# The start of a list-scheduled kernel ordered by a stored table of ranks

## The chip, the cores and the metric

The kernel runs on one core of a Trainium2 chip. The core has five engines, each of which takes its own instructions strictly in order: TensorE (PE in the profile; PEld is its loading of weights), VectorE (DVE), ScalarE (ACT), GpSimd (POOL) and SyncE (SP), which issues the transfers here. The metric is the device time of one execution in microseconds (us), the median of several runs.

## The reference

Linear attention with a random feature map, then a two-layer feed-forward network over all tokens. B = H = 8, S = 576, head dimension 64, 128 features; 4608 tokens of 512 channels, a hidden width of 2048; all inputs and the output are float32.

```
def phi(x):
    proj = np.einsum('bhsd,df->bhsf', x, w_phi)
    proj = proj - np.max(np.abs(proj), axis=-1, keepdims=True)
    return np.concatenate([np.exp(proj), np.exp(-proj)], axis=-1)
q_p, k_p = (phi(q), phi(k))
kv = np.einsum('bhsf,bhsd->bhfd', k_p, v)
z = np.sum(k_p, axis=2)
num = np.einsum('bhsf,bhfd->bhsd', q_p, kv)
den = np.einsum('bhsf,bhf->bhs', q_p, z)[..., None] + 1e-06
x = (num / den), tokens x (H * D)
h = x @ w_in;  r = np.maximum(h, 0.0);  out = (r * r) @ w_out
```

## The kernel before

**The work.** The attention runs in 32 pairs of heads of one batch, four pairs to a batch (`NPAIR`). The feed-forward part, called MoE in the code, runs in 18 chunks of 256 tokens by 8 steps of 256 hidden channels. A step has a first GEMM (24 matmuls, L986, into a bank pair `ph`), a chain of ReLU and square on ACT (L995, L997, L999) and a subtraction on DVE that makes a high part `gh` and a low part `gl`, and a second GEMM (12 matmuls, L1013, into `po`). A chunk can start when the normalized tokens of its batches are in `ring0` or `ring1`, as a high and a low half (L804 on ACT, L807 on DVE).

**The weights.** `w_in` and `w_out` come in eight blocks each as raw 64-bit data, 1 MB a block (`raw0i` to `raw7i` for `w_in`, `raw0o` to `raw7o` for `w_out`). `prep` turns a block into float32 `u` and then into halves: ACT L453 and L448, DVE L456 and L460; for a block of `w_in` also the largest value on ACT (L477), a power of two as its scale (`power`: a transposing gather on TensorE, L402, into the bank `pn`, then four small steps on DVE, L406 to L410), and the halves `win0` (ACT L481) and `win1` (DVE L483); for a block of `w_out` the halves `wh` (ACT L501) and `wl` (POOL L313 and DVE L508). A raw buffer is reused for a later block, so its load waits on SP until the earlier one was read.

**The first six pairs** (0 to 5, `early`) run before there are tokens for the MoE steps. For a pair p TensorE projects k (L563 for the main part, into banks `po` for pairs 0 to 4 and `pp` for pair 5; L569 for the tail, into `pn`) and q (L680 and L686). DVE finds the largest values and subtracts them (`km`, `e`, `kmt`, `et`: L579, L582, L589, L592; for q `qm`, `pt`: L691, L693), ACT takes the exponentials (L585, L587, L595, L597). TensorE multiplies k's features with v (L619, L624, sums in L652, into `pv`); ACT or DVE copies the result out as `kvs` (L317 or L318), TensorE flips it (L664), the flipped copy is `kz`. TensorE flips q's features in two halves (L714, L718, into `pp`), ACT takes their exponentials `qe` (L723, L725), TensorE makes the numerators (L733, copied out as `n`) and denominators (L750, copied into `sx`). The denominators go by a transfer from `sx` to `den`, DVE takes the reciprocal (L767, L768, `rc`), which goes through memory (`rd`) and back spread over all rows (`rb`); DVE multiplies numerators with `rb` (L785). The later pairs run as one `visit` each among the MoE steps.

**Buffers.** PSUM has one `pn`, one `pv`, one `pp` (two banks), two `ph`, two `po`. One buffer `sx` in SBUF serves the copies of the denominators and, as a place for unwanted output, ACT's L526, which sums |v| for the scale of a batch. So the next user of such a buffer waits until all users of the last one are done, a transfer included.

**The order.** All of this is given as operations to a planner (`Plan`), each with an engine (some with a second engine), a duration, what it depends on, the buffers it uses and a rank. `order` is a list scheduler: it goes through a modelled time and gives each engine that is free the ready operation of the least rank (TensorE adds `STAY` to one that would change its tiling). The order of their modelled starts is the order in which the instructions are then written, engine by engine. The core of it:

```
t = free[e] if ready[e] else max(free[e], waiting[e][0][0])
if best is None or t < best[0]:
    best = t, e
...
if e == "PE":
    pick = min(ready[e], key=lambda x: (x[0] + (STAY if self.ops[x[1]].mode[0] != mode else 0.0), x[1]))
    ready[e].remove(pick)
    op = self.ops[pick[1]]
else:
    op = self.ops[heapq.heappop(ready[e])[1]]
```

Ranks come from the code: a pair p has `PER_PAIR * p` (4.5 p) plus a small number for the place in the pair, block n of the weights `PREP0 + PREP1 * n` (16 + n), MoE step n has `LEAD + n` (36 + n); the MoE work on ACT and DVE has its rank less 1000, which puts it ahead of all else. `improve` takes the 1113 operations with ranks between -50 and 70 (the pairs up to about 15, all weights, the GEMMs of about the first 34 steps), moves the ranks of a twentieth of them at random, makes the order anew and keeps it if the modelled end is no later; it does this 400 times from a fixed seed.

Of the kernel before, what the change touches and what calls it, by code (L numbers as in the profile page):

```python
# [3 lines left out]

# [22 lines left out]
B, H, S, D = 8, 8, 576, 64  # L27
F = 128
NP = H // 2
NPAIR = B * NP  # L30
DM = 512
# [4 lines left out]
T = 256  # L36
# [12 lines left out]
STAY = 6.0  # L49
LATER = 2.0  # L50
BEHIND = 0.0
TRIALS, SEED, MOVED = 400, 1, 70.0
CHANGE = 0.15
RA, RQ, RZ = 1.3, 0.4, 0.3
COLD = 1.15
# [22 lines left out]
class Plan:  # L78
# [59 lines left out]
                    todo.append(a)  # L138
        return False

    def improve(self, trials, seed):

        rnd = random.Random(seed)
        best, plan = None, None
        some = [op for op in self.ops if -50.0 < op.rank < MOVED]
        for n in range(trials):
            moved = rnd.sample(some, len(some) // 20) if n else []
            old = [(op, op.rank) for op in moved]
            for op in moved:
                op.rank += rnd.gauss(0.0, 1.5)  # L150
            order = self.order()
            length = max(op.end for op in self.ops)
            if best is None or length <= best:
                best, plan = length, [(op, op.eng) for op in order]
            else:
                for op, rank in old:
                    op.rank = rank
        for op, eng in plan:
            op.take(eng)
        return [op for op, _ in plan]  # L160

    def order(self):
        for op in self.ops:
# [136 lines left out]
def tile_kernel(ctx, tc, qp, kp, vp, w_phi, w_in, w_out, out):  # L300
    nc = tc.nc
    V, A, G, PE, SP = nc.vector, nc.scalar, nc.gpsimd, nc.tensor, nc.sync
    P = Plan()
# [747 lines left out]
    for p in range(NPAIR):  # L1051
        if p % NP == 0 and p:
            b = p // NP
# [16 lines left out]
        op.after = [x for a in op.after for x in (chunk_done[a[1]] if isinstance(a, tuple) else [a])]  # L1070
    P.close()
    with tc.manual_schedule():
        for op in P.improve(TRIALS, SEED):
            op.fn()


PREP0, PREP1 = 16.0, 1.0
# [27 lines left out]
```

## Time and profile before

| what | value |
|---|---|
| median of 3 runs | 1076.79 us (1075.55 to 1077.38) |
| span of the profiled execution, first to last instruction | 1074.5 us |
| mean granted TensorE clock | 0.986 |
| busy: PE, PEld, DVE, ACT, POOL | 1038.8, 707.2, 738.3, 635.6, 136.4 us |

The profiled execution is known by its span; the median of the runs is 2.3 us above that span. A line of a profile gives the engine, the line of the program, the tile that is written and those that are read, and the idle time ahead of it with what ended it. The line numbers are those of the kernel before. PE's records overlap, so a busy PE means only that it has something in flight; the granted clock (1.00 is full speed) is given by stage.

### The profile page before, as it was taken

The numbers are of one execution on the slowest core, as the hardware profiler recorded it, in microseconds if no ns is written. First come the engines' busy times: TensorE is split into PE (matmuls) and PEld (weight loads), VectorE is DVE, ScalarE is ACT, GpSimd is POOL, SyncE is SP. The second block draws the span as 40 slices with busy tenths as digits, with TensorE's granted clock in tenths as the row PEclk, the third lists the DMA queues.
The fourth block names the chain that finished last, engine by engine and source line by source line (L and its number), as shares of the span: only waits on it lengthen the run. The fifth ranks groups of instructions, "written<-read, shape, count | busy, mean of one in ns | idle before, by whom it ended". The sixth has DMA issues, their size and how long they took to land.

```text
span 1074.5 us, 19722 instructions
## 1 busy us (share of the span) xinstructions
PE 1038.8 (97%) x7762; PEld 707.2 (66%) x7762; DVE 738.3 (69%) x1558; ACT 635.6 (59%) x1132; POOL 136.4 (13%) x66
## 2 busy tenths in 40 slices
PE   7778899999999999999999999999999999999997
PEld 5545566666666666666666666666666666677674
DVE  6688988788868877878878877777787855112111
ACT  6789876666656665656665655666556645333332
POOL 0012211111111111111111101111110111000000
PEclk9988999999999999999999999999999999999998
DMA  9742422131122122222212121112120101000000
GB/s 319 272 136 86 163 91 60 29 95 45 59 58 85 45 76 56 76 56 66 67 56 76 56 62 43 52 52 76 44 63 23 51 13 41 1 20 20 1 20 20
DMA packets 68289, 73.49 MB, mean 68 GB/s; under 512 B 36836, under 2 KB 41828, under 8 KB 68196
## 3 DMA queue, kind: packets, MB, share of 16 engines
q1 hardware_dynamic: 68196, 72.23, 22.0%
q8 instruction: 61, 1.00, 0.4%
q14 instruction: 32, 0.26, 0.1%
HBM read 59.18 MB, written 12.99 MB: 67 GB/s over the span
## 4 chain that ended last, share of the span: by engine, by line
PE 90%; DVE 5%; DMA 3%; issue 1%; ACT 0%; SPq 0%; DVEq 0%; ACTq 0%
PE po L1013 37%; PE ph L986 35%; PE pv L619 5%; PE pp L563 3%; PE pn L837 3%; PE pp L907 3%; PE pv L837 2%; PE pv L624 1%; PE pn L569 1%; DVE wl L508 1%; DMA den<-sx 1%; DMA k<-in_kp_dram 1%; DMA v<-in_vp_dram 1%; DMA rd<-rc 1%; DVE u L460 1%
## 5 line engine op out<-in xcount | busy, mean ns | idle before, releaser
L986 PE MATMUL ph<-ring,win 128*128 128x256 f16 x3456 | 398.1, 273 | 0.0
L986 PEld LDWEIGHTS <-win 128*128 128x128 f16 x3456 | 335.8, 98 | 66.2 <-issue 5.4
L995 ACT ACTIVATE r<-ph,cw 128x512 f32<-128x512 f32 x144 | 98.8, 686 | 221.1 <-PE ph L986 221.0
L313 DVE TENSOR_TENSOR gl<-ph,gh 128x512 bf16<-128x512 f32 x144 | 98.5, 684 | 168.0 <-ACT ph L999 167.4
L920 POOL PARTITION_ALL_REDUCE mx<-pt x52 | 114.2, 2197 | 621.5 <-ACT pt L317 449.9
L1013 PE MATMUL po<-wh,gh 128*128 128x512 f32 x432 | 129.4, 421 | 0.0
L1013 PE MATMUL po<-wl,gh 128*128 128x512 bf16 x432 | 112.8, 384 | 0.0
L1013 PE MATMUL po<-wl,gl 128*128 128x512 bf16 x432 | 110.9, 379 | 0.0
L1013 PEld LDWEIGHTS <-gl 128*128 128x128 bf16 x576 | 56.1, 97 | 69.8 <-issue 0.4
L997 ACT ACTIVATE gh<-r 128x512 fp32r<-128x512 f32 x144 | 90.7, 630 | 6.2 <-PE po L1013 1.7
L1013 PEld LDWEIGHTS <-gh 128*128 128x128 bf16 x576 | 44.9, 98 | 74.7 <-issue 40.3
L1013 PEld LDWEIGHTS po<-wh,gh 128*128 128x128 f32 x432 | 74.5, 190 | 18.7 <-issue 5.4
L999 ACT ACTIVATE ph<-r 128x512 f32<-128x512 f32 x144 | 84.0, 583 | 0.1
L1013 PE MATMUL po<-wout,gh 128*128 128x512 f32 (+1 forms) x288 | 75.8, 404 | 0.0
L317 ACT ACTIVATE n<-pn 128x320 f32<-128x320 f32 (+1 forms) x32 | 13.8, 431 | 100.7 <-PE pn L837 98.4
L619 PE MATMUL pv<-e,v 128*64 128x256 f32 x512 | 63.9, 394 | 0.7 <-ACT kz L317 0.7
L934 DVE SCALAR_TENSOR_TENSOR pt<-qe,zc,pt 128x576 f32<-128x576 f32 x52 | 42.2, 812 | 18.9 <-ACT pt L932 18.2
L313 DVE TENSOR_TENSOR qe<-pt,mx 128x576 f32<-128x576 f32 x52 | 39.2, 755 | 16.8 <-POOL mx L920 16.5
L619 PEld LDWEIGHTS pv<-e,v 128*64 128x64 f32 x512 | 36.9, 142 | 17.8 <-issue 3.6
L585 ACT ACTIVATE e<-e 128x512 f32<-128x512 f32 x64 | 39.7, 621 | 14.6 <-DVE e L582 14.4
L925 ACT ACTIVATE qe<-qe 128x576 f32<-128x576 f32 x52 | 34.9, 671 | 13.9 <-DVE qe L313 13.9
L871 DVE STREAM_TRANSPOSE kvs<-pv 128x256 f32<-128x256 f32 x26 | 11.6, 445 | 44.3 <-PE pv L837 42.4
(206 smaller groups left out, 1394.0 us busy)
## 6 DMA issues: line engine op xcount, KB each, us to landing
v<-in_vp_dram SPq DMA_DIRECT2D x32, 320.0 KB
k<-in_kp_dram SPq DMA_DIRECT2D x32, 288.0 KB
q<-in_qp_dram SPq DMA_DIRECT2D x32, 288.0 KB
rb<-rd SPq DMA_DIRECT2D x64, 144.0 KB
out_dram<-o SPq DMA_DIRECT2D x36, 256.0 KB
td<-kvs SPq DMA_DIRECT2D x26, 128.0 KB
kz<-td SPq DMA_DIRECT2D x208, 16.0 KB
raw0i<-in_w_in_dram SPq DMA_DIRECT2D x1, 1024.0 KB
```

What stands on the lines that cost most here:

```text
L313: eng.tensor_tensor(out=out_, in0=a, in1=b_, op=ALU.subtract)
L585: o = P.add("ACT", act_us(512), lambda n=n: A.activation(out=e_[n][:, :, 1, :], in_=e_[n][:, :, 0, :], func=AF.Exp, scale=-1.0), [o], [("e ...
L619: PE.matmul(out=to[64 * h:64 * h + 64, 0:256], lhsT=v_[p][:, t, h, :], rhs=e_[2 * p + h][:, t].rearrange("p s f -> p (s f)"), start=t == 0 ...
L837: PE.matmul(out=to[64 * h:64 * h + 64, :], lhsT=kz_[n][:, 128 * s_ + 64 * h:128 * s_ + 64 * h + 64], rhs=qe_[2 * n + h].rearrange("p (s x) ...
L920: o = P.add("POOL", par_us(S), lambda n=n, h=h: G.partition_all_reduce(mx_[n], pt_[p][:, h, :], channels=128, reduce_op=bass_isa.ReduceOp. ...
L925: o = P.add("ACT", act_us(S), lambda qe=qe: A.activation(out=qe(1), in_=qe(0), func=AF.Exp, scale=-1.0), [o], [("qe", n)], R(RQ + 0.4))
L934: o = P.add("DVE", dve_us(S), lambda h=h, qe=qe, y=y: V.scalar_tensor_tensor(out=y(), in0=qe(1), scalar=zc_[p][:, 2 * h + 1:2 * h + 2], in ...
L986: PE.matmul(out=ph[:, j, :], lhsT=win[w][:, t, 128 * ff:128 * ff + 128], rhs=ring[half][x][:, t, c0:c0 + T], start=k == 0, stop=k == 3 * K ...
L995: o = P.add("ACT", act_us(512, 1), lambda: A.activation(out=r_[n], in_=ph_[bank], func=AF.Relu, scale=cw[:, f, 0:1]), [g1], [("ph", bank), ...
L997: sq = P.add("ACT", act_us(512), lambda: A.activation(out=gh_[n], in_=r_[n], func=AF.Square), [o], [("r", n), ("gh", n)], Q)
L999: o = P.add("ACT", 0.59, lambda: A.activation(out=ph_[bank], in_=r_[n], func=AF.Square), [o], [("ph", bank), ("r", n)], Q, other=("DVE", 0 ...
L1013: PE.matmul(out=po_[po[i][1]], lhsT=g[:, j, 128 * i:128 * i + 128], rhs=w[:, j, :], start=(ff == 0 and s == 0), stop=(ff == 2 * NFP - 1 an ...
```

## The change

`improve` no longer searches. It reads one rank for each of the same 1113 operations from a string of 2226 characters, two to a rank in base 90, with a step of 0.05, and calls `order` once. Nothing else of the plan changes: the operations, their modelled durations, what they depend on and the buffers are the same, so the same work is done in another order on each engine, and a few operations that may run on either of two engines change sides (ACT has 1091 rows for 1094, DVE 1299 for 1298). The table of 23 lines is cut to its first here.

```
--- before.py
+++ after.py
@@ -1,5 +1,4 @@
 import heapq
-import random
 from contextlib import ExitStack
 
 import numpy as np
@@ -49,7 +48,7 @@
 STAY = 6.0
 LATER = 2.0
 BEHIND = 0.0
-TRIALS, SEED, MOVED = 400, 1, 70.0
+MOVED = 70.0
 CHANGE = 0.15
 RA, RQ, RZ = 1.3, 0.4, 0.3
 COLD = 1.15
@@ -138,26 +137,14 @@
                     todo.append(a)
         return False
 
-    def improve(self, trials, seed):
-
-        rnd = random.Random(seed)
-        best, plan = None, None
+    def improve(self):
+
         some = [op for op in self.ops if -50.0 < op.rank < MOVED]
-        for n in range(trials):
-            moved = rnd.sample(some, len(some) // 20) if n else []
-            old = [(op, op.rank) for op in moved]
-            for op in moved:
-                op.rank += rnd.gauss(0.0, 1.5)
-            order = self.order()
-            length = max(op.end for op in self.ops)
-            if best is None or length <= best:
-                best, plan = length, [(op, op.eng) for op in order]
-            else:
-                for op, rank in old:
-                    op.rank = rank
-        for op, eng in plan:
-            op.take(eng)
-        return [op for op, _ in plan]
+        assert 2 * len(some) == len(RANKS)
+        for n, op in enumerate(some):
+            i, j = (DIGITS.index(x) for x in RANKS[2 * n:2 * n + 2])
+            op.rank = (90 * i + j - 3000) * 0.05
+        return self.order()
 
     def order(self):
         for op in self.ops:
@@ -1070,8 +1057,36 @@
         op.after = [x for a in op.after for x in (chunk_done[a[1]] if isinstance(a, tuple) else [a])]
     P.close()
     with tc.manual_schedule():
-        for op in P.improve(TRIALS, SEED):
+        for op in P.improve():
             op.fn()
+
+
+DIGITS = "".join(chr(c) for c in range(33, 127) if chr(c) not in "\"\\'")[:90]
+RANKS = (
+    "E*I*6};p:FN}3lBSJ8;JD3V-JRBNL&_`XLL^L|OOIhRkK8>VJ&MY[.B)F/SJ>GP{3oD)JXPwHgIUJiayZ#RAP(OxL6OeU>DiI:Sy"
...
+)
 
 
 PREP0, PREP1 = 16.0, 1.0
```

In the new kernel the lines up to the scheduler's end stand 13 lower: its L304 is L317 of before, its L513 is L526. The rows below are those of the two orders; a name ends in a number of its own for each buffer, and the number ahead of it counts the pair (`e_6` and `e_7` are the two heads of pair 3) or the use.

First place: ACT, in the start, around the second denominators' copy into `sx` (`sx_6` before, `sx_5` now) and the copy `kvs_2` that the flip of pair 2 waits for. Before:

```order
L453 ACTIVATE raw0o_364<-raw0o_364 128x1024
L317 ACTIVATE sx_6_570<-pn_9_535 128x288
L585 ACTIVATE e_6_533<-e_6_533 128x4x128
L587 ACTIVATE e_6_533<-e_6_533 128x4x128
L526 ACTIVATE sx_7_587,vm_1_531<-v_5_405 128x640
L317 ACTIVATE kvs_2_593<-pv_5_508 128x384
L723 ACTIVATE qe_4_598<-pp_4_580 128x2x288
L585 ACTIVATE e_7_591<-e_7_591 128x4x128
L725 ACTIVATE qe_4_598<-pp_4_580 128x2x288
```

The same place on ACT now:

```order
L304 ACTIVATE sx_5_541<-pn_8_500 128x288
L710 ACTIVATE qe_4_545<-pp_4_521 128x2x288
L572 ACTIVATE e_6_543<-e_6_543 128x4x128
L574 ACTIVATE e_6_543<-e_6_543 128x4x128
L712 ACTIVATE qe_4_545<-pp_4_521 128x2x288
L488 ACTIVATE wh0_585<-u_2_528 128x1024
L435 ACTIVATE u_3_593<-raw2i_419 128x1024
L304 ACTIVATE kvs_2_611<-pv_5_532 128x384
L572 ACTIVATE e_7_609<-e_7_609 128x4x128
L574 ACTIVATE e_7_609<-e_7_609 128x4x128
L440 ACTIVATE raw3o_285<-raw3o_285 128x1024
L304 ACTIVATE kz_2_639<-pv_6_635 128x384
```

Before, an L526 for v_5 (`sx_7`) stands three rows behind the copy into `sx` and ahead of `kvs_2`. Now `kvs_2` stands seven rows behind the copy, and the next L526 (for v_4, `sx_6`) follows only behind the last row shown.

Second place: DVE, in the start, around the reading of the second denominators (`den_1`) and `e_7`, which frees the bank `po_7` that the projection of pair 4 writes next. Before:

```order
L582 TENSOR_TENSOR e_6_533<-po_6_489,km_6_524 128x4x128
L579 TENSOR_REDUCE km_7_545<-po_7_491 128x4
L460 SCALAR_TENSOR_TENSOR u_3_517<-u_3_517,raw2i_288 128x1024
L456 SCALAR_TENSOR_TENSOR raw0o_364<-raw0o_364 128x1024
L582 TENSOR_TENSOR e_7_591<-po_7_491,km_7_545 128x4x128
L460 SCALAR_TENSOR_TENSOR u_2_487<-u_2_487,raw0o_364 128x1024
L785 TENSOR_TENSOR rb_0_572<-n_0_392,rb_0_572 128x576
L767 TENSOR_SCALAR den_1_576<-den_1_576 128x9
L768 RECIPROCAL rc_1_618<-den_1_576 128x9
```

The same place on DVE now:

```order
L569 TENSOR_TENSOR e_6_543<-po_6_481,km_6_519 128x4x128
L447 SCALAR_TENSOR_TENSOR u_2_528<-u_2_528,raw0o_361 128x1024
L678 TENSOR_REDUCE qm_2_457<-pn_9_555 128x1
L680 TENSOR_TENSOR pt_2_474<-pn_9_555,qm_2_457 128x128
L754 TENSOR_SCALAR den_1_549<-den_1_549 128x9
L755 RECIPROCAL rc_1_589<-den_1_549 128x9
L495 CAST wl0_586<-u_2_528 128x1024
L569 TENSOR_TENSOR e_7_609<-po_7_483,km_7_530 128x4x128
L772 TENSOR_TENSOR rb_0_551<-n_0_351,rb_0_551 128x576
```

`e_7` has gone from ahead of `rb_0` and `den_1` to behind `den_1`, its reciprocal and the cast of `wl0`; the cast stood nine rows behind `den_1` before.

Third place: ACT, ahead of the first MoE step, around the two reads of the flipped second half of pair 4's q (`qe_9`), which free the banks `pp`. Before:

```order
L481 ACTIVATE win0_76<-u_5_808,cw_81 128x4x256
L317 ACTIVATE n_3_956<-pv_13_986 128x288
L501 ACTIVATE wh2_1003<-u_6_898 128x1024
L477 ACTIVATE raw4i_415,wm_4_108<-u_7_961 128x1024
L723 ACTIVATE qe_9_1010<-pp_9_995 128x2x288
L448 ACTIVATE u_8_1012<-raw3o_480 128x1024
L509 ACTIVATE wl2_1004<-u_6_898 128x1024
L804 ACTIVATE ring0_0_78<-rb_3_982,cb_82 128x576
L725 ACTIVATE qe_9_1010<-pp_9_995 128x2x288
```

And the same place on ACT now:

```order
L513 ACTIVATE sx_12_967,vm_2_968<-v_8_771 128x640
L435 ACTIVATE u_6_975<-raw2o_816 128x1024
L468 ACTIVATE win0_76<-u_5_866,cw_81 128x4x256
L304 ACTIVATE n_3_986<-pn_22_979 128x288
L440 ACTIVATE raw4o_946<-raw4o_946 128x1024
L435 ACTIVATE u_7_1002<-raw4i_517 128x1024
L304 ACTIVATE n_3_986<-pv_13_991 128x288
L710 ACTIVATE qe_9_1016<-pp_10_1004 128x2x288
L572 ACTIVATE e_11_988<-e_11_988 128x4x128
L712 ACTIVATE qe_9_1016<-pp_10_1004 128x2x288
```

Before, four passes over a block of weights (`win0`, `wh2`, `raw4i`, `u_8`) and a fifth (`wl2`) stand among these rows, and what PE puts into `pp` next is pair 5's k. Now an L526, the next user of `sx` after the fourth denominators, stands first, and four passes over weights (`u_6`, `win0`, `raw4o`, `u_7`) ahead of the first read of `qe_9`. On PE pair 5's k has moved ahead of this flip, and what comes into `pp` next is pair 5's q, which stood behind the first first-GEMM of a MoE step and now stands ahead of it.

More of the change, by code (lines that the diff above doesn't have):

```diff
@@ L1072, in tile_kernel @@
     with tc.manual_schedule():
-        for op in P.improve(TRIALS, SEED):
+        for op in P.improve():
             op.fn()
+DIGITS = "".join(chr(c) for c in range(33, 127) if chr(c) not in "\"\\'")[:90]
+RANKS = (
+    "E*I*6};p:FN}3lBSJ8;JD3V-JRBNL&_`XLL^L|OOIhRkK8>VJ&MY[.B)F/SJ>GP{3oD)JXPwHgIUJiayZ#RAP(OxL6OeU>DiI:Sy"
+    "O{X,`oTMPGRtZ3JqY{;k;ADoSfPv7VQH:2UgU^MZ`@ZYItKLiTPH^WpO^!KBE@Uo:IClI<M*SQQ9VgR2EsC(;TQoZ5U$O|5+?K1w"
+    "CVKrJ2QTCO:M%+#P?Y02#-7c#-#-#-#-#-523i;?=v<(:7d1c)_QbEMrJ{EO<cPq?/8i(w5.8A>!61&?LeV&Sr<^0p@/8DBO::(8"
+    "./>_GTDO7j8Q2$W524+>2<>F82*q.!8j,>=@Ep7zbZ>-4>.B>E9H;^8mE[D98B2<+E1d*Z*z.A/..?+x-14@&z0G6!$8C(&z;5.2"
+    "/S/s0s8n61<v6X=e9!0X=F8L@N<f=-$Y7UHr2n5s2|*M,^7p>.>+*O3T&9(,(!7s(B(V(t%T&%0;)H)5.G&L(?(=6e*&01,QD>^q"
+    ";ZX/G+IXMxEM;q<?<V8$;,Pi5vI|A@I>=>@)@LPJ7;A&MN+6&x7Y/mBDCM;C=V@iH>@MN3>*I$6%AiA7Goe6NDZT>oIVO1OH.G*d"
+    "I&D9103c<+5d2b=[DAD-8qEcP4ICNOB)>AG*N??cRd>sO6FBH534C`E#:k-JAaGS@CBX2!6.M$-p8sBT;[:bR]GUQ`MkB-BYO_QM"
+    "QUIhI-RaB9G|Q]RBJm=bKpO7R{>]H/N(Mu7_<&5[?DKnB)K>L{aGR;LmOhWgUtB_>G9c??3(),>?:`EmHM>5HPR}V5_ld7[of(Qe"
+    "NAR)TwQ@G:TwVST{YRR;WM]aS#UX`9U3Ih;ETcT/THSUA*WUEoJFNdK8V$L_TnF,DXFD?CDrIM7^DL>5<%A%N9Tm?z?<N8EzKAAH"
+    "V7]qXBGT`yM6Z@tU_KouR-RpSwGjH+>W*ORY:b8Y9{5xAt@?@DREHp:|@7,+>xB2J0<3MI9}>?:|H`inc-LtZiPg7(1@<@<JM]Ou"
+    "JWO{NdW|Z2<dLXcgLSPe^ec4duYev5Z4F-lm]DPuKsU.z>X`{LWrf0V98Y7UDs]wbXY0`,]9goh{PERAfJcS^ZMDe:esPxm@fPMu"
+    "Oj[$XAawYoY%_sEkFd?p>CEV?zIQT_KCE8^pLWOZF!_&K(fieR_z`3R)T)]0cV^4SOAMD[m#FQXC^Pn*YE^J`CUMLRIgR]APR@-z"
+    "R{L%;59BMD;v5UEL$}>c0kO!Ft1lD}>r>jF]?=A1LyKA>k?mM7QEJ&.g@mZgZ*Z(EgEPI.Z$AJ)n7[HJ%{0p(46p3S,2Bs=^8FJm"
+    "92a#JZ^i^3e!YZq.NOv`TFI9UiSlh4QV;9q!E;_PGrMQEFK8PcKjUdk(vPi[k{u/d}[cZ[UiL2Y,g|j/d+afe3chH(h[_yNBc:Ry"
+    "K<NvQ_BfU-Fn<d_%PC`<o3M!m`hhVSa^i7lt|2dVV%k&c.j[lQjDb{r5VGY(`$N0Zzd@XfY,M}Gw<fLiC*APE[MFG2Y@:1I/SDe_"
+    "hm`;Vb<UV&[VAj>6=k:I@|<GC`<Q&O*g%D4o&y4,0S-d({&*2G1X*y/8>c<`@EID3!DM)>#.)^1?FCJsIzIDAo^A@3FtO{P}StDH"
+    "Kp_f=HI[MBI:0-KX-e>KAbD]N!_*S7@94e8!5h2(0t-g(s-B-Y0D/*0e4VD70D<U%3.N*X2j4_3!645XVk8UWTP<V:WUBILbKBC}"
+    "J>A>OV/3<R6!*>+9O5MHF5JqMP4{=I:2FOQhD27I@$QBCK%7,8<M)$:58Z8d5I7wHJ#-#-0}5,2E#5%6/h-W$Q%51A,?.I5U>.7o"
+    "Br:l76CLT2H-FhQ]Bk=:FR7>X9L%UxFoW`SDm&p0Q6[:rrTnpBg&ZSKdK@CN?iApC-_,>{2%@xCQ1@4L%K&9,.5h6z:l+=/u$XF7"
+    "%b.^0k4v8YPAYgl,_;jDdRuIyJ|LvCjmX+eFZJIU8kGA;g`iLS]QRsED/_&l@[9//L@N7]O3P%WkWLRjLDOkL^b1PK:$[QlqljgC"
+    "g>U|hVYvRR@4J]RBA<&PD8[0=g@GDW;ZMUCwA(6=>sBFA}7U/;9y:lDx[pQ!`nH@G_5ZD<LCGjMi@sL8eynejWl{VUGCNcNoNR??"
+    "H|VCegNxMf]9V8R.MKT/P1VAekjLbwX6WJSwbFc9Xk_8c`c`ZWVaC7Mh7OL+f>UU]+c8]lJ6UdTGW3S(IAbU=vSlTBQ^cNo0^@N:"
+    "O^Y_W0U|i*[5FKPmWB[NKaM.EK"
+)
```

## The prediction

> **What bounds the kernel now.** First the page: the span, TensorE's share, and TensorE over the 40 slices (27 us each).
>
> ```profile
> span 1074.5 us, 19722 instructions
> PE 1038.8 (97%) x7762; PEld 707.2 (66%) x7762; DVE 738.3 (69%) x1558; ACT 635.6 (59%) x1132; POOL 136.4 (13%) x66
> PE   7778899999999999999999999999999999999997
> ```
>
> TensorE is the bound, and is short of work only in the first slices and the last. Busy time by stage says where (columns: length, busy us per engine, granted clock, DMA share, GB/s):
>
> ```profile
> 0.00:50.00 50.00, 36.87 (x413) 26.19 (x415) 32.45 (x65) 35.33 (x66) 0.68 (x6) 0.95 0.88 312
> 50.00:100.00 50.00, 37.93 (x371) 23.67 (x370) 41.31 (x69) 43.89 (x74) 7.50 (x3) 0.84 0.34 104
> 100.00:125.00 25.00, 21.94 (x188) 14.86 (x187) 24.35 (x39) 23.60 (x36) 6.18 (x2) 0.93 0.52 165
> 125.00:1066.60 941.60, 941.60 (x6799) 642.54 (x6796) 638.58 (x1385) 532.77 (x960) 122.02 (x55) 1.00 0.18 51
> 1066.60:1074.50 7.90, 0.47 (x3) 0.00 (x0) 1.62 (x2) 0.00 (x0) 0.00 (x0) 0.65 0.17 67
> ```
>
> From 125.0 to 1066.6 TensorE never idles and has its full clock. Idle before that is 13.1 + 12.1 + 3.1 = 28.3 us; the last 7.9 us are the output's way out. The amount of TensorE work is fixed, so the time can move only by waits before 125 us, by the clock there, or by a new wait later. The waits of TensorE up to 135 us, in us, count and longest:
>
> ```profile
> PE po L563 <- DMA k<-in_kp_dram: 6.3, 2, 4.3
> PE pv L664 <- ACT kvs L317: 4.6, 1, 4.6
> PE pn L733 <- DVE et L592: 4.5, 1, 4.5
> PE pn L402 <- DVE pw L406: 3.0, 1, 3.0
> PE pn L750 <- DVE pw L406: 2.2, 1, 2.2
> PE pp L714 <- ACT qe L725: 2.1, 2, 1.5
> PE pn L402 <- DVE et L592: 1.4, 2, 1.0
> ...
> PE pv L619 <- ACT kz L317: 0.7, 1, 0.7
> PE pn L402 <- DVE m L531: 0.7, 1, 0.7
> ...
> ```
>
> The first row (loads of the first two keys) comes before anything that the table can move: the first nine loads are issued in the same order in both. The other 22.0 us are waits of in-order engines. Each long one is followed by a stretch at a lower granted clock:
>
> ```profile
> 23.50:28.00 4.50, 3.97 (x22) 2.26 (x24) 4.36 (x12) 4.14 (x7) 0.00 (x0) 0.62 1.02 375
> 48.40:52.60 4.20, 4.08 (x35) 3.56 (x35) 1.32 (x3) 4.20 (x9) 0.00 (x0) 0.59 0.20 60
> 74.10:79.60 5.50, 5.44 (x36) 2.69 (x38) 2.90 (x6) 3.60 (x4) 0.00 (x0) 0.54 0.79 238
> 91.90:97.00 5.10, 5.07 (x32) 3.18 (x32) 1.65 (x3) 3.88 (x7) 0.00 (x0) 0.57 0.02 3
> 119.90:123.70 3.80, 3.75 (x11) 2.08 (x12) 3.43 (x11) 3.29 (x5) 0.00 (x0) 0.55 0.73 248
> ```
>
> Busy time times the missing clock: 1.5 + 1.7 + 2.5 + 2.2 + 1.7 = 9.6 us, 1.9 per wait. So 22.0 + 9.6 = **31.6 us** could be moved.
>
> **What goes.** Two long waits, by their rows (chain, ACT, DVE):
>
> ```profile
> 31.77 4.51 DMA den<-sx
> 43.38 3.77 DMA den<-sx
> 47.23 0.74 ACT L526 ACTIVATE sx<-v 128x640 bf16<-128x640 f32 x1 [4.50 <-DMA den<-sx]
> 88.98 2.60 DVE L785 TENSOR_TENSOR rb<-n,rb 128x576 f32<-128x576 f32 x1 [0.23 <-DMA rb<-rd]
> ```
>
> ACT's L526 may not write the one buffer sx before the transfer of the second denominators has read it. The copy kvs_2 stands behind it on ACT, and TensorE's flip waits 4.6 us for kvs_2. The new order puts kvs_2 ahead of L526 and twelve instructions between the copy into sx and L526, so that wait goes. In the second, et_4 stood behind the product rb_3 on DVE; now et_4 stands ahead even of rb_2. The other three long ones (3.0, 2.2, and 0.7 + 0.7) are waits of TensorE for the bank pn, held until DVE has run a power's four small steps or the tails (L402 to L410, L589 to L592). In the new order m1_0's gather comes a pair later and wm_4 to wm_7 stand behind the first two second GEMMs. I take all 31.6 us as gone and price the new order's waits afresh.
>
> **What comes.** I laid the new rows of PE, ACT, DVE and SP beside each other up to the seventh first-GEMM. Each row starts when its engine is free and its last producer is done, with its line's duration, and loads land in order at the GB/s of their stage. These waits are left. More rows for them (a landing, stages, sizes, durations):
>
> ```profile
> 14.34 7.33 DMA v<-in_vp_dram
> 13.50:25.00 11.50, 10.08 (x125) 7.12 (x125) 10.12 (x23) 10.30 (x21) 0.00 (x0) 0.98 0.97 346
> 25.00:43.90 18.90, 18.13 (x231) 11.82 (x227) 14.04 (x25) 15.84 (x29) 0.00 (x0) 0.92 1.02 373
> v<-in_vp_dram SPq DMA_DIRECT2D x32, 320.0 KB
> q<-in_qp_dram SPq DMA_DIRECT2D x32, 288.0 KB
> raw3o<-in_w_out_dram SPq DMA_DIRECT2D x1, 1024.0 KB
> 60.22 1.16 PE L680 MATMUL ph<-wraw,q 64*128 64x128 f32 x16
> 62.33 1.90 PE L619 MATMUL pv<-e,v 128*64 128x256 f32 x16
> 54.14 1.48 DVE L508 CAST wl<-u 128x1024 bf16<-128x1024 f32 x1
> 71.29 2.52 DVE L508 CAST wl<-u 128x1024 bf16<-128x1024 f32 x1
> L481 ACT ACTIVATE win<-u,cw 128x1024 f16<-128x1024 f32 x7 | 8.0, 1147 | 2.2 <-DVE cw L410 2.2
> L585 ACT ACTIVATE e<-e 128x512 f32<-128x512 f32 x12 | 7.5, 626 | 0.1
> ```
>
> - (a) ACT converts raw3i early and has kvs_1 behind it. The fourth v lands at 14.34 + 7.33 = 21.7; behind it in the queue are raw3o, v_4, q_2 and raw3i, 2.7 MB, at 346 to 373 GB/s 7.5 us: raw3i lands at 29.2, where ACT, in that layout, comes to it at 27.4. The flip of kvs_1 waits **1.7**.
> - (b) The reading of den_1 stands on DVE ahead of wl0 and e_7, and k_4's projection needs e_7's bank. From the end of pair 1's denominators (L750) to k_4 TensorE has 6.1 us of work (1.9 + 1.16 and about 3 of small pieces). sx_5, the copy of those denominators, is written 1.2 us into that stretch, once ACT is through with u_2; the transfer takes 4.2 (mean of 4.51 and 3.77), den_1 and its reciprocal 0.4, wl0 between 1.48 and 2.52 (nearer the latter, as GpSimd makes wl0's other half then), e_7 0.6: 8.9 to 9.1. TensorE waits **3.0**; nothing else is in its queue to hide it.
> - (c) wm_0's gather waits for n_1, which stands on ACT behind ring0 and two L526: **1.3**.
> - (d) Around wm_2 the bank pn passes through four owners, with den_2 ahead of et_4: 0.6 + 1.1 + 0.3 = **2.0**.
> - (e) pair 3's numerators wait for wm_3's power, then a flip for e_11: **2.1**.
> - (f) q_5's projection needs the bank that both reads of qe_9 free. From the copy of den_3 into sx to L526, which must wait for that transfer, ACT has 2.1 us of rows and waits 0.5 more; from L526 to the second read stand ten instructions, four of 128x1024 at about 1.05 apart, L526's 0.73, three of 0.5 to 0.6 and two small ones: 7.2 us. So the bank is free 9.8 us after the copy, and TensorE has 6.5 us of work and waits (e) in that time: **3.3**.
> - (g) the passage to the MoE steps: **1.2**.
>
> Sum 14.6; (b) and (f) are of the kind that lowers the clock, 1.9 each: 3.8. Waits of some tenths can't be seen in such a list; before has 2.8 us in the rows left out above, so I add **2.0**. Together 20.4. Gain 31.6 - 20.4 = 11.2, on the span 1074.5 to 1063.3. The median of the runs is 1076.79, 2.3 us above the span, so 1065.6; I say **1066**. After 125 us the table moves MoE steps too, but the cover stays: before the third chunk's first GEMM stand three second GEMMs (8 us) behind the last numerators of batch 1, where before there were two and a projection, without a wait. Further on the pairs stand a MoE step or two to one side of where they stood, in the same pattern.
>
> [...]
>
> **The rivals.**
>
> 1. *ACT sets the pace.* TensorE's waits are then only symptoms, and what is gained is the time that ACT stood still for avoidable reasons: 4.50 (above) and the 2.1 us that L804 waited for rb. Then 1076.8 - 6.6 = 1070. For it: ACT's idle time to 125 us is only 50 - 35.3 + 50 - 43.9 + 25 - 23.6 = 22 us, and 6.4 of them are waits for the first loads of v. Against it: the clock's 9.6 us are no work of ACT's. 26%.
>
> ```profile
> ACT sx L526 <- DMA v<-in_vp_dram: 6.4, 2, 5.5
> ...
> ACT ring L804 <- DVE rb L785: 2.1, 1, 2.1
> ```
>
> 2. *Short waits keep the clock*: (b) and (f) then cost 6.3 and not 10.1: 1062. The five stretches above speak against it. 10%.
> 3. *Slower: the early pairs are used up before the weights are done.* In the new order the first MoE step stands behind nearly all of pair 5; beside the first five steps only 4 us of its work are left, where before there were about 10. A step whose two weights are still to be converted costs ACT four and about three 128x1024 passes, 1.15 each, and 2 us of its own, some 9 us against TensorE's 5.5. If weights 4 to 7 are all late that is 4 x 3.5 = 14 us: 1080. It turns slower when more than three of them are late. Against it: at the first step ACT has by its rows about 40 us of work up to the last weight, TensorE 53. 7%.
> 4. *Nothing to measure*: if the transfers of den_0 to den_3 land 2.8 us later each than I took them (4.2, later 2.6), and DVE or ACT stands before each, 4 x 2.8 = 11.2 us are given back: 1077. Against it: the longest of the rows above is 4.51. 7%.
>
> That the order stays as it was is out: the rows differ from the second flip on.
>
> **How the numbers follow.** The forecast, 1062.5 to 1069.5, has 50%, the rivals 26, 10, 7 and 7. A change under 0.2% (2.2 us) can't be told from none. Faster: 50 + 26 + 10 = 86%; same 7%; slower 7%. The range takes in the clock rival below and ACT's pace above, with wl0 and den_1 at their ends (2 us): 1060 to 1073.
>
> **What would show it.** The flip of kvs_2 and et_4's reader without a wait; TensorE's idle time to 125 us near 20 instead of 28, with waits for e_7's bank and for qe_9 of about 3 us each; full clock outside two stretches; nothing but 100% from 130 us to the end. It is wrong if TensorE idles after 130 us, or if many waits of 1 us stand where I have none.

## The result, and the profile after

| | before | changed |
|---|---|---|
| median of the runs | 1076.86 us (1075.55 to 1077.38) | 1071.25 us (1070.10 to 1072.56) |
| span of the profiled execution | 1074.5 us | 1068.7 us |

The ratio is 0.995, with a 95% interval of 0.9935 to 0.9964: 5.6 us faster, between 4 and 7. The forecast of 1066 had the sign and the bound right and promised twice the gain (10.8 us below the median before). 1071.25 lies outside the forecast's 1062.5 to 1069.5 and inside its outer bounds of 1060 to 1073. Runs of one kernel spread over some 3 to 9 us, so below medians are set beside medians, and rows beside rows. One run each of `no_shifts` (1101.67 us), `den3_first` (1190.96) and `warm` (2160.20) lies far above its fellows for a reason that stays open, and the medians and ratios below leave these three out.

The stages of the kernel before, cut anew (columns as in the prediction; first the length, then TensorE's busy time; the granted clock is the figure behind POOL's):

```profile
13.50:125.00 111.50, 89.59 (x914) 58.64 (x914) 91.88 (x157) 96.39 (x163) 13.68 (x5) 0.89 0.56 188
125.00:1000.00 875.00, 875.00 (x6355) 596.22 (x6351) 628.22 (x1371) 511.08 (x924) 122.02 (x55) 1.00 0.19 54
1000.00:1074.50 74.50, 67.07 (x447) 46.32 (x445) 11.98 (x17) 21.69 (x36) 0.00 (x0) 0.96 0.04 15
```

The page of the changed kernel, its span and busy times:

```profile
span 1068.7 us, 19712 instructions
...
PE 1037.3 (97%) x7762; PEld 706.9 (66%) x7762; DVE 740.5 (69%) x1561; ACT 635.1 (59%) x1129; POOL 135.3 (13%) x66
```

TensorE is the bound as before, with as much work. The same stages of the changed kernel:

```profile
13.50:125.00 111.50, 95.64 (x981) 63.83 (x978) 90.75 (x162) 97.85 (x164) 14.12 (x6) 0.92 0.54 179
125.00:1000.00 875.00, 872.44 (x6319) 594.19 (x6317) 632.38 (x1370) 510.17 (x921) 120.53 (x55) 1.00 0.19 55
1000.00:1068.70 68.70, 62.43 (x414) 42.86 (x412) 11.45 (x16) 20.34 (x34) 0.00 (x0) 0.98 0.04 16
```

From 13.5 to 125 us TensorE's idle time falls from 21.9 to 15.9 us, and busy time times the missing clock from 89.59 x 0.11 = 9.9 to 95.64 x 0.08 = 7.7 us: 8.2 us are won there. From 125 to 1000 us there are 2.6 us of idle time where there were none, and the last stretch idles 6.3 us for 7.4. Ahead of 13.5 us TensorE idles 0.3 us longer. 8.2 - 2.6 + 1.1 - 0.3 = 6.4, and the spans differ by 5.8; the granted clock is printed to 0.01, which is up to 0.5 us in each of the two products. The clock ahead of 13.5 us can't be compared: the traces hold no clock record before 14.3 us (before) and 7.7 us (changed), and the view prints 1.00 where there is none. The first 16 matmul rows of a key projection take 2.08 us in both kernels there, against 1.16 us later at full clock.

TensorE's waits in the changed kernel (us in total, times, longest):

```profile
PE po L550 <- DMA k<-in_kp_dram: 6.6, 2, 4.1
PE po L550 <- DVE e L569: 3.0, 1, 3.0
PE pp L667 <- ACT qe L712: 2.8, 1, 2.8
PE pv L651 <- DVE kvs L305: 2.5, 1, 2.5
PE po L1000 <- DVE o L1011: 2.5, 2, 1.6
PE pn L720 <- DVE pw L393: 1.6, 1, 1.6
PE ph L973 <- DVE gl L300: 1.3, 1, 1.3
PE pv L651 <- ACT kvs L304: 1.2, 1, 1.2
...
```

The waits of 4.6 and 4.5 us are gone as foretold, and those on e_7's bank and on qe_9 are there at nearly the price given. The one on L1011 stands at 564 and 622 us. These rows of SP, DVE and PE show the first:

```profile
557.82 3.65 SPq L864 DMA_DIRECT2D kz<-td  x8
561.57 0.38 SPq L1014 DMA_DIRECT2D out_dram<-o  x1
...
555.65 0.79 DVE L1011 TENSOR_SCALAR o<-po,cc 128x512 f32<-128x512 f32 x1
563.75 0.81 DVE L1011 TENSOR_SCALAR o<-po,cc 128x512 f32<-128x512 f32 x1 [4.46 <-DMA out_dram<-o]
...
564.61 0.73 PE L1000 MATMUL po<-wh,gh 128*128 128x512 f32 x2 [1.57 <-DVE o L1011]
```

The first of a chunk's two outputs is in `o` at 556.4 us. Its store stands on SP behind eight transfers of `kz` that wait for `td`, and goes out at 561.6. There is one `o`, so DVE's second output waits 4.46 us for that store, keeps its bank `po`, and the next chunk's second GEMM waits for the bank.

### The profile page after: what moved, and what is told of

Read it like the earlier page. It is cut to its first block, busy times and chain, and to the rows that moved or that the text cites. A ratio compares the mean times of both kernels' runs of the same rounds, so it can differ in the third digit from the quotient of the medians.

```text
span 1068.7 us, 19712 instructions
## 1 busy us (share of the span) xinstructions
PE 1037.3 (97%) x7762; PEld 706.9 (66%) x7762; DVE 740.5 (69%) x1561; ACT 635.1 (59%) x1129; POOL 135.3 (13%) x66
## 4 chain that ended last, share of the span: by engine, by line
PE 86%; ACT 5%; DMA 4%; DVE 3%; SPq 2%; issue 1%; DVEq 0%; ACTq 0%
PE po L1000 35%; PE ph L973 33%; PE pv L606 4%; PE pp L550 2%; PE pn L824 2%; PE pp L894 2%; PE pv L824 2%; DMA den<-sx 1%; SPq L864 1%; PE pv L611 1%; PE pn L556 1%; DMA raw3i<-in_w_in_dram 1%; DMA out_dram<-o 1%; DMA k<-in_kp_dram 1%; DMA td<-kvs 1%
## 5 line engine op out<-in xcount | busy, mean ns | idle before, releaser
L304 ACT ACTIVATE n<-pn 128x320 f32<-128x320 f32 (+1 forms) x32 | 13.8, 430 | 72.2 <-PE pn L824 70.1
L1011 DVE TENSOR_SCALAR o<-po,cc 128x512 f32<-128x512 f32 x36 | 28.7, 798 | 25.4 <-DMA out_dram<-o 19.2
```

## The experiments

The theory to test was the prediction's own, with the late wait added: TensorE's waits and the clock behind them add up, and each can be taken away by itself. The rival was that a wait taken away comes back at the next operation that is fed late. The moves by hand act on `plan`, the list of operations in order of their modelled starts; names such as `("inv", 1)` (den_1 and its reciprocal) stand for operations of the plan.

```
+        plan = P.improve()
+        def behind(a, b): # a, and what stands between and depends on it, behind b
+        def ahead(a, b):  # a, and what stands between and it depends on, ahead of b
-        for op in P.improve():
+        for op in plan:
```

**Two output tiles** (`o_two`: the changed kernel; `before_o_two`: the kernel before, its order untouched).

```
-    o_ = tiles(mp, "o", [128, DM], F32, 1)
+    o_ = tiles(mp, "o", [128, DM], F32, 2)
+    P.bufs["o"] = 1
```

> The new kernel with two buffers for o, the finished output tile, instead of one; the order of all instructions is the same. Theory (the two waits of second GEMMs for the copy into o, 1.6 and 0.9 us at 564 and 622 us, are a new cost of the new order, since the store of the first tile stands behind eight transfers of kz on SyncE): those waits go and the time falls by 2.5 us, to 1068.7. Rival (the cover elsewhere takes it: something else is late by as much): within 0.5 us of 1071.

> The kernel before, its order of instructions unchanged, with two output tiles o in place of one. Theory (the one output tile made the changed order wait late, at 564 and 622 us, and the order before it did not have these waits; both orders have the 2.15 us of the second output behind the first one's store at the end): the kernel before gains only its tail, 2 to 3 us: 1073.8 to 1074.8 us. Against the changed kernel with two output tiles (1064.8 us) the table alone is then worth 9 to 10 us. Rival (the second tile is worth as much here as there, by something else than the waits at 564 and 622 us): about 6.5 us, 1070.3 us, and the table is worth 5.5 us with either.

Measured: 1064.76 us with the table (1062.97 to 1066.15; ratio 0.9884, 0.9867 to 0.99) and 1073.49 without (0.9979, 0.9968 to 0.9991). (The last line keeps the planner's count at one, so that the order stays as it is.) With the table and two tiles, the late stretch:

```profile
125.00:1000.00 875.00, 875.00 (x6343) 596.61 (x6342) 633.84 (x1371) 510.35 (x920) 120.55 (x55) 1.00 0.19 55
```

And DVE's last row there:

```profile
1058.20 1.53 DVE L1012 TENSOR_SCALAR o<-po,cc 128x512 f32<-128x512 f32 x2 [2.48 <-PE po L1001]
```

TensorE is full again, and the last two outputs run back to back; in the changed kernel the last one waited 2.15 us for the store ahead of it. That second effect was missing from the first expectation. The kernel before gains only it, 2.8 us. So beside two output tiles the table is worth 11.9 - 2.8 = 9.1 us (10.2 by the ratios), where it is worth 5.6 with one: 3.5 us or more of the forecast gain went into this wait. The two profiled runs with the table agree: their instructions stand in the same order, and ACT's ReLU row (one to a step) that starts at 519.12 us with one tile starts 0.4 us earlier with two, the one at 806.51 us 3.8 us earlier.

**The search alone** (`no_shifts`: the kernel before with `TRIALS` 1 in place of 400, that is, the ranks as the code gives them).

> The kernel before with no random shifts at all: the ranks as the code gives them, one pass of the scheduler. It tells what 400 shifts bought on the chip, next to what the table buys. Theory (each step of a search on the planner's model brings some part on the chip): slower than the kernel before by 4 to 12 us, so 1081 to 1089, through more idle time of TensorE before 130 us. Rival (what the model gains is mostly lost on the chip): within 3 us of 1077.

Measured: 1077.98 us, ratio 1.0014 (1.0001 to 1.0027). Its longest wait is 8.3 us:

```profile
PE pn L734 <- DVE et L593: 8.3, 1, 8.3
```

The kernel before has no wait of that length, so the 400 random shifts had moved the order; the time they moved by 1.5 us, with an interval of 0.1 to 2.9.

**den_1 read later** (`e7_first`, `inv1_late`). The first puts e_7 alone ahead of the reading of den_1 on DVE, the second all three operations for k's features of pair 3.

```
+        ahead(("e", 7), ("inv", 1))
```
```
+        behind(("inv", 1), ("et", 3))
```

> The new kernel with one step moved on VectorE: e_7 (the subtraction that frees the bank of pair 4's k projection) stands ahead of the reading of den_1 instead of three places behind it. Theory (in-order wait of 3.0 us plus the slow clock behind it, 2.9 us): the 3.0 us wait of L550 goes and the time falls by 4 to 6 us, to 1065 to 1067. Rival (ScalarE sets the pace): the fall is no more than the 3.4 us that ScalarE waited for the same e_7, so 1068 or above; if DMA landings set the pace, nothing, 1071.

> The changed kernel; on DVE the reading of den_1 and its reciprocal stand behind e_7, kmt_3 and et_3 in place of ahead of them, and the store of rd_1 moves two loads later on SP. Theory: both waits of TensorE that hung on the transfer den_1 go, the 3.0 us of pair 4's key projection and the one on et_3 that took its place when e_7 alone was moved, and with them the clock of 0.52 behind them, which costs 3.1 us: 1065 to 1067 us. Rival (the wait only moves on again, to the next thing behind the transfer or to ACT, whose exponentials of e_7 are late anyway): 1069.5 to 1071 us, with a new wait of 2 us or more before 60 us.

Measured: 1070.69 us (0.9941, 0.9926 to 0.9956) and 1070.42 us (0.9949, 0.9932 to 0.9967): 0.5 and 0.8 below the changed kernel, no difference that can be told. In the first the wait of 3.0 us became this one:

```profile
PE pn L722 <- DVE et L581: 3.3, 1, 3.3
```

In the second, rows of DVE and PE:

```profile
45.78 0.76 DVE L781 TENSOR_TENSOR rb<-n,rb 128x576 f32<-128x576 f32 x1 [4.00 <-DMA rb<-rd]
...
47.68 2.19 PE L728 MATMUL pn<-qe,kz 128*64 128x288 f32 x8 [3.39 <-DVE den L763]
```

DVE, freed from den_1, stands 4.00 us for the next transfer, rb_0: it is there at 45.8 us, where den_1 had been read at 44.3 in the changed kernel. My theory that the order on DVE was the cause fell here: both transfers are late together.

**The load ahead of them** (`raw4i_late`): only the 1 MB load of raw4i moves, behind den_1 and rb_0 on SP.

```
+        behind(("ld", 4, True), ("rb", 0))
```

> The changed kernel with one transfer moved on SP: the 1 MB load of raw4i is issued behind den_1 and rb_0, two issues later, in place of ahead of them; nothing else moves. Theory (the wait of 3.0 us at pair 4's key projection is the load: den_1, 4.5 KB, and rb_0 are queued behind 1.3 MB of loads of which raw4i is 1 MB, and DVE, which works in order, stands until they land, whichever operation is put first there): den_1 lands about 3 us sooner, DVE's 4.26 us of idle time shrink to 1.5 or less, the 3.0 us of TensorE go and the clock of 0.52 behind them with them (3.1 us): 1065 to 1067 us. Rival (ACT or DVE, nearly full before 125 us, set the pace, and the time comes back as other waits, as when den_1 was read later): 1069.5 to 1071 us with a wait over 2 us elsewhere before 70 us.

Measured: 1069.55 us (1067.85 to 1073.62; 0.9937, 0.9921 to 0.9952). The changed kernel, SP and DVE:

```profile
35.84 0.42 SPq L426 DMA_DIRECT2D raw4i<-in_w_in_dram  x1
37.88 0.59 SPq L745 DMA_DIRECT2D den<-sx  x1
...
44.26 0.17 DVE L754 TENSOR_SCALAR den<-den 128x9 f32<-128x9 f32 x1 [4.26 <-DMA den<-sx]
```

With raw4i behind, SP, DVE and PE:

```profile
38.59 0.58 SPq L754 DMA_DIRECT2D den<-sx  x1
40.84 0.59 SPq L428 DMA_DIRECT2D raw4i<-in_w_in_dram  x1
...
40.64 0.16 DVE L763 TENSOR_SCALAR den<-den 128x9 f32<-128x9 f32 x1
...
45.98 1.19 PE L728 MATMUL pn<-qe,kz 128*64 128x288 f32 x8 [1.24 <-DVE et L584]
```

The 4.5 KB of den_1 took 6.4 us from issue to use behind the 1 MB, and at most 2.05 us without it. The wait at k_4 went, so the load was its cause. What it is worth is less sure. The median is 1.7 us below the changed kernel's where some 6 were expected, and the intervals overlap (0.9921 to 0.9952, and 0.9935 to 0.9964), so these runs do not tell the gain from none. The profiled run, the fastest of its six, is 2.9 us shorter. From 13.5 to 125 us it idles 15.4 us for 15.9: in place of the 3.0 us stand new waits of 0.2 to 1.2 us before 64 us, the longest of them in the row shown. It has three stretches of 3.41 us at half clock after 15 us, where the changed kernel has five. So the waiting came back at the next late operations. Some of the clock did not, but two profiles of one order differ by nearly as much (below, at the clock).

**Filling the wait** (`warm`, `warm_once`, `warm_half`): matmuls that change no output, in TensorE's waits. `warm` has 66 in four places, the others 28 and 12 ahead of pair 4's key projection alone.

```
-        km = P.add("PE", 1.1, lambda: k_main(p, k_to), ...
+        km = P.add("PE", 1.1, lambda: k_main(p, k_to, 4 if p == 4 else 1), ...
```

> The new kernel, with TensorE kept busy in its three longest early waits: 20 repeats of the first head's matmuls of pair 4's k projection (they write the same values again) ahead of the matmul that waits for e_7's bank, and 17, 10 and 19 spare 128x128 matmuls into a bank of ph not yet in use ahead of pair 4's flip, pair 3's numerators and pair 5's q projection. No wait is removed, nothing is computed otherwise. Theory (the lost part is the clock, which each wait halves for the next 6 us or so, in all 7 us): 1071 less 5 to 7, so 1064 to 1066, with TensorE's granted clock near 1.00 from 45 to 95 us. Rival (ScalarE sets the pace, the slow clock only fills time that would be waited anyway): within 1 us of 1071, the waits only move to other places.

> The changed kernel with 28 matmuls of 128 by 128 more (work that changes no output) ahead of the key projection of pair 4, in the 3.0 us that TensorE waits there for e_7; 14 such took 1.0 us at full clock, so they fill about 2 us of the 3. Theory (the granted clock of 0.52 from 45.8 to 52.3 us is the price of that wait): the stretch behind it runs at full clock and the kernel gains up to 3.1 us: 1068 to 1069.5 us, with no longer wait behind it. Rival 1 (what TensorE does faster there it waits for afterwards, since ACT sets the pace): 1071 us, the stretch at full clock and new waits behind it before 70 us. Rival 2 (the clock falls all the same, as the remaining 1 us is enough): 1071 us and a clock under 0.7 there.

> The changed kernel with 12 matmuls more (24 rows of the trace; work that changes no output) ahead of pair 4's key projection, in TensorE's 3.0 us wait for e_7. With 28 of them the 72 rows took 7.41 us in place of 1.16 for 16, 0.11 us each, and overran the wait by over 3 us; 24 rows take 2.7. Theory (the clock of 0.52 after the wait is its price and is gained by itself): the wait falls to 0.5 us or less, the stretch from 45.8 to 52.3 us runs at full clock, the first GEMM of the MoE starts up to 3 us sooner, 1068 to 1069.5 us. Rival 1 (what is done faster there is waited for right behind it): full clock there, but as much more waiting before 61 us as clock gained, 1070.5 to 1071.5 us. Rival 2 (the clock falls all the same): under 0.7 there, 1071 us.

Measured: 1074.67 (0.998, 0.9967 to 0.9993), 1075.76 (0.9995, 0.9979 to 1.0012) and 1075.90 us (0.9999, 0.9985 to 1.0013), all 3 to 5 us above the changed kernel. In `warm_once` the dose was wrong:

```profile
45.13 7.41 PE L549 MATMUL po<-wraw,k 64*128 64x128 f32 x72
```

The usual 16 rows, which alternate between the two heads, take 0.073 us each; mine, all of one head, took 0.11, so 56 of them overran the wait, and at that rate `warm`'s 40 rows there did too. Neither says what the clock is worth. With 24 rows (`warm_half`) the dose is right. Rows of PE:

```profile
43.43 3.90 PE L549 MATMUL po<-wraw,k 64*128 64x128 f32 x40
...
51.84 0.49 PE L389 MATMUL pn<-ident,wm 128*128 128x128 f32 x2 [1.82 <-ACT n L304]
```

The busy times there in stretches of 3.41 us (TensorE's first, its clock behind POOL's):

```profile
49.75:53.17 3.42, 1.60 (x13) 0.91 (x12) 3.38 (x6) 3.39 (x11) 0.00 (x0) 1.00 0.19 61
53.17:56.58 3.41, 3.41 (x26) 2.47 (x24) 3.25 (x9) 3.35 (x6) 0.00 (x0) 0.50 0.00 0
```

The wait is filled, the clock stays at 1.00 to 53 us, and TensorE then stands 1.82 us for n_1 (the wait (c) of the prediction, which the changed kernel did not have), and is at half clock from 53.2. From 13.5 to 125 us it has 16.0 us of idle time and 7.6 of missing clock, as the changed kernel had, and 2.7 us of filling beside them. So far rival 1 holds: what TensorE does faster here it waits for at the next operations.

That does not explain the whole time, which is 4 us above rival 1's. ACT's ReLU row that starts at 519.12 us in the changed kernel starts 2.4 us later here, about the filling; the one at 806.51 starts 7.4 us later, and the spans differ by 7.5. The other 5.0 us come with the late wait for the one output tile (L1011 of the changed kernel, L1010 here):

```profile
PE po L999 <- DVE o L1010: 6.0, 3, 3.2
```

That is 6.0 us for 2.5, and from 400 to 700 us the mean granted clock is 0.99 for 1.00. Why it is longer at the same order of instructions is open. The profiled run is 2.3 us above the median of its kernel.

**The transfer den_3** (`den3_first`): issued ahead of the 1 MB of raw4o, in place of right behind it.

```
+        ahead(("den", 3), ("ld", 4, False))
```

> The changed kernel with the transfer den_3 (4.5 KB) issued ahead of the 1 MB load of raw4o on SP, where it stood right behind it; nothing else moves. Theory (den_3 landed 5.4 us after its issue for the load ahead of it; ACT stood 1.30 us for it ahead of the work that leads to qe_9's reads, and TensorE's 2.8 us at pair 5's query projection hang on those): den_3 lands within 3 us, ACT's 1.30 us go, TensorE's wait falls to 1.5 us, with less clock lost behind it: 1068.5 to 1070.5 us. Rival (ACT's time until qe_9 is set by its work, so that raw4o, landing later, takes the place of den_3): the wait stays at 2.5 us or more, 1071 us.

Measured: 1070.69 us, ratio 0.9951 (0.9929 to 0.9972), which can't be told from the changed kernel. Rows of ACT and PE:

```profile
77.52 0.74 ACT L517 ACTIVATE sx<-v 128x640 bf16<-128x640 f32 x1
81.14 1.19 ACT L442 ACTIVATE raw4o<-raw4o 128x1024 int32<-128x1024 uint32 x1 [0.39 <-DMA raw4o<-in_w_out_dram]
...
85.33 2.08 PE L673 MATMUL pp<-wraw,q 64*128 64x128 f32 x16 [3.25 <-ACT qe L719]
```

ACT's 1.30 us of waiting for den_3 are gone, and TensorE waits 3.25 us for qe_9 all the same. ACT's work between the copy of den_3 and the reads of qe_9 sets that wait, not the transfer; the rival holds.

**All together** (`four_moves`, `two_loads_late`, both with two output tiles).

```
+        behind(("inv", 1), ("et", 3))                 # four_moves only
+        ahead(("kvs", 4), ("mul", 2))                 # four_moves only
+        ahead(("bits", 4), ("win1", 2))               # four_moves only
+        behind(("ld", 4, True), ("rb", 0))            # two_loads_late only
+        ahead(("den", 3), ("ld", 4, False))           # both
+        ahead(("num", 3, 1), ("low", 4, False))       # both
+        ahead(("q1", 9), ("low", 4, False))           # both
+        ahead(("q2", 9), ("low", 4, False))           # both
```

> The changed kernel with two output tiles and four moves by hand, each at a place where TensorE waited over 2 us: den_1 behind e_7, kmt_3 and et_3 on DVE; the transfer den_3 ahead of the load of raw4o on SP; the second numerator of pair 3 and the reads of qe_9's bank ahead of the work on raw4o on ACT; kvs_4 ahead of the product of rb_2 and of the weights' win1 on DVE. Theory (the waits and the clock behind them are the sum; two output tiles give 1064.8): less 3.0 on den_1, 2.8 on qe_9, 2.5 on kvs_4 and about 4 of clock: 1053 to 1057 us. Rival (each wait gives way to the next late operation, as when e_7 alone was moved, since the engines that feed TensorE are nearly full before 125 us): 1061 to 1064 us.

> The changed kernel with two output tiles, the load of raw4i behind den_1 and rb_0, the transfer den_3 ahead of the load of raw4o, and on ACT the second numerator of pair 3 and the reads of qe_9's bank ahead of the work on raw4o; DVE keeps its order. Theory (two output tiles give 1064.8; the wait on den_1 with its clock is worth 4 to 6 us, that on qe_9 2.8 us and as much of clock): 1057 to 1060 us. Rival (the waits move on, as with the four moves): 1063 to 1065 us.

Measured: 1065.93 us (0.9908, 0.9889 to 0.9928) and 1063.10 us (1060.53 to 1064.97; 0.9878, 0.9864 to 0.9892). The four moves bring nothing that can be told over the second output tile (the line on `bits` takes block 4's small steps on DVE along, ahead of win1). Their three longest waits behind those for the first keys:

```profile
PE pn L729 <- DVE den L764: 3.2, 1, 3.2
PE pp L708 <- DVE e L574: 2.8, 1, 2.8
PE pn L747 <- DVE et L585: 1.9, 1, 1.9
```

The first is the one that `inv1_late` had. The waits on qe_9 and kvs_4 went; the last two, on e and et, are new. `two_loads_late`, which takes a load out of the way in place of changing DVE's order, has the lowest median of all kernels here, but its interval overlaps that of `o_two` (0.9867 to 0.99). Both beat the kernel before and the changed one.

## Why the prediction was wrong in its size, step by step

- **What goes.** That all of the old waits after 13.5 us go held: no L526 ahead of kvs_2, no product ahead of et_4.
- **What comes.** Right in size, and partly by luck: 14.6 + 2.0 = 16.6 forecast, 15.9 of idle time measured, with one wait missing from the list and one that did not come. By place (forecast, measured): (a) 1.7, 1.2; (b) 3.0, 3.0; (c) 1.3, none; (d) 2.0, 0.8 + 0.9; (e) 2.1, 1.6; (f) 3.3, 2.8; (g) 1.2, 1.3. The flip of kvs_4, 2.5 us, was not in the list; kvs_4 stands on DVE behind the product of rb_2, for whose transfer DVE stood 2.89 us. Two reasons were wrong where the sums were right: (b) took the transfer of den_1 at 4.2 us (it was over 6, behind the load of raw4i, and wl0's cast took 0.63 us for the 2.5 or so that I took: GpSimd's pass for the other half, 2.36 us from 41.14, was over when it started at 44.60, where the rows of 1.48 and 2.52 us of the kernel before stand beside such a pass, at 52.63 to 55.08 and 70.91 to 73.26 us), and (f) was ACT's own work and needed no late den_3.
- **The clock: the step that failed first.** The term was "(b) and (f) are of the kind that lowers the clock, 1.9 each: 3.8". It measured 7.7 us. In the trace of the changed kernel the record of the granted clock starts at 7.70 us, and each of its changes up to 93.03 us (11.11, 14.52, 45.24, 52.07, 79.38, 82.79, 86.20, 93.03) stands a whole number of 3.41 us behind that; in between it is 1.00 or 0.50. The changed kernel in this grid:

```profile
41.82:45.24 3.42, 1.05 (x12) 0.57 (x8) 0.94 (x4) 0.66 (x2) 1.68 (x1) 1.00 0.60 159
45.24:48.65 3.41, 2.77 (x17) 2.28 (x17) 2.25 (x5) 2.28 (x3) 0.00 (x0) 0.50 0.60 164
48.65:52.06 3.41, 3.41 (x15) 1.67 (x14) 2.02 (x3) 3.21 (x9) 0.00 (x0) 0.50 0.35 106
...
75.95:79.37 3.42, 0.55 (x3) 0.31 (x3) 3.42 (x6) 2.28 (x3) 0.00 (x0) 1.00 0.88 306
79.37:82.78 3.41, 2.86 (x12) 1.48 (x14) 3.31 (x9) 2.61 (x4) 0.00 (x0) 0.50 0.11 38
82.78:86.19 3.41, 1.86 (x16) 0.90 (x12) 3.05 (x6) 3.41 (x7) 0.00 (x0) 1.00 0.17 24
86.19:89.61 3.42, 2.20 (x20) 1.98 (x24) 3.32 (x4) 3.39 (x9) 0.00 (x0) 0.50 0.43 153
89.61:93.02 3.41, 3.41 (x24) 1.36 (x20) 3.41 (x7) 2.06 (x5) 0.00 (x0) 0.50 0.00 0
```

  A window in which TensorE was busy 1.05, 0.55 or 1.86 us of 3.41 is followed by one at 0.50, and one at 0.50 in which it was busy 2.77 or 2.20 us by a second at 0.50; with 2.86 it went back to 1.00. Five windows at half clock cost (2.77 + 3.41 + 2.86 + 2.20 + 3.41) / 2 = 7.3 us. I counted two waits at 1.9; there were three places, for kvs_4's and wm_3's waits (2.5 and 1.6 us, neither over my 3) fell into one window, and two of the three places took two windows. My "full clock outside two stretches" is wrong by that third place. The order alone does not fix the size: `o_two`, with the same order and the grid at another phase (an edge at 66.62 us, where the changed kernel has one at 65.71), has four such windows from 15.41 us on, which by the same count cost (3.41 + 3.41 + 0.23 + 3.41) / 2 = 5.2 us. Both are above 3.8.
- **After 125 us: the second step that failed.** "But the cover stays" and "nothing but 100% from 130 us to the end". I looked at the first GEMMs and the numerators, and not at the stores on SP, which the table moves too. It cost 2.5 us in the rows, 3.5 or more between the pairs of kernels with one and two output tiles. Some of "the output's way out" was also a wait for the same tile, 2.15 us in both orders.
- **The sum.** 0.7 less waiting than forecast, 7.7 - 3.8 = 3.9 more clock, 2.6 more late idle time, 1.1 less at the end and 0.3 more before 13.5 us: 11.2 + 0.7 - 3.9 - 2.6 + 1.1 - 0.3 = 6.2, for 5.8 between the spans; the rest is within the rounding of the clock.
- **The rivals.** *ACT sets the pace* named 1070 and came nearest, but not by its mechanism: the stretch to 125 us gave 8.2 us, more than its 6.6, and two output tiles give 9.1. What is true in it is that TensorE's early waits are handed on: of five attempts to take one away, two moved it (`e7_first`, `inv1_late`), one filled it for nothing (`warm_half`), one left it (`den3_first`), and one (`raw4i_late`) broke it up into shorter ones, with a gain that the runs do not tell from none. But ACT is not alone in setting them: (b) hung on DVE's wait of 4.26 us for a transfer. *Short waits keep the clock* fell: no wait of TensorE behind the first loads is longer than 3.0 us, and half clock was granted from 45.24 to 52.06 us, beginning inside (b)'s wait (42.87 to 45.88), and from 86.19 to 93.02 us, beginning inside (f)'s (84.64 to 87.41). One of the five stretches that spoke against it was read wrongly in part: in the kernel before the clock fell at 72.35 us, inside the wait of 2.2 us (71.98 to 74.16) and not after it, behind a window (68.94 to 72.35) with 2.01 us of work. *Weights late* did not happen (by its own terms seven passes of 1.15 and 2 us are 10 us a step, not 9, so 18 us for four and not 14). *Nothing to measure* did not either; the transfers of den_1 and den_3 were later by 2 to 3 us, as the last supposed, but they were two and not four.

Open: that a wait taken away comes back is shown for these places only. Neither `raw4i_late` against the changed kernel nor `two_loads_late` against `o_two` is told apart by these runs. What makes the late wait longer in `warm_half` is not known.

## What to carry to other kernels

Where the bound engine is fed by several in-order engines, list its waits with their neighbours and the transfers behind them: taking one away is worth its length only if the next operation on the same chain is on time, so price the chain and not the wait. Look at what a new order does to every queue, the stores included, through to the end: a buffer with a single copy ties the end of one chunk to the start of the next, and a second copy was the cheapest gain here. The clock was priced better here by windows (five of them, 7.3 us of the 7.7 measured) than by waits (3.8 us).

## What the runs showed of the hardware

- In eleven profiles (all but those of `warm`, `four_moves` and `before_o_two`), laid out in 33 windows of 3.41 us each from 14 to 17 us on, the granted clock of every window is 0.50 or 0.51, or else 0.99 or 1.00. Of the windows at full clock there, all 28 with 1.69 us or less of TensorE work were followed by half clock, none with 2.13 us or more was, and between them both occur (1.86 us kept the clock in the kernel before, at 55.28 us, and lost it in the changed one, at 82.78). Two waits of 0.8 and 0.9 us show what the grid's phase does. In the changed kernel they fall into two windows and cost nothing more; with two output tiles they fall into one, and the next runs at half clock:

```profile
62.30:65.71 3.41, 2.14 (x18) 1.21 (x15) 2.58 (x10) 3.41 (x7) 0.00 (x0) 1.00 0.19 31
65.71:69.13 3.42, 2.86 (x24) 1.89 (x24) 3.38 (x8) 3.10 (x6) 0.00 (x0) 1.00 1.05 409
```
```profile
63.21:66.62 3.41, 1.65 (x16) 1.21 (x16) 2.72 (x9) 3.09 (x6) 0.00 (x0) 1.00 0.69 233
66.62:70.04 3.42, 3.42 (x20) 1.97 (x18) 3.32 (x8) 3.42 (x5) 0.00 (x0) 0.50 0.68 252
```

  By the count above (half of its busy time) a window at half clock costs up to 3.41 / 2 = 1.7 us, so two profiles of one order can differ by some us for their phase alone (7.3 and 5.2 us above). That this makes part of the spread between runs of one kernel is likely but not shown, as each kernel has one trace.
- A transfer of 4.5 KB (den_1) behind 1 MB (raw4i) in the same queue took 6.4 us from issue to use in the changed kernel, and at most 2.05 us ahead of it in `raw4i_late`.
- A granted clock of 1.00 can mean that there is no record: the kernel before has none up to 14.3 us, the view prints 1.00 from 0 to 13.5, and the first 16 rows of a key projection take 2.08 us there, against 1.16 later at full clock. In `warm` the view prints 1.00 over the whole length, while a first GEMM's matmul takes 443 ns on the mean, where the changed kernel has 273 ns, and the execution took 2160.2 us. The cause is open.
